# First block's scores from on-chip operands over 64 rows each, and six search steps planned among the weight conversions

## Chip, core and metric

One core of one Trainium2 chip runs the whole program. The metric is the device time of one execution in microseconds (us); smaller is better. The engines are called as the profile calls them: PE (TensorE), ACT (ScalarE), DVE (VectorE), POOL (GpSimd), and SP (SyncE), which here issues every DMA. A profiled execution supplies the trace.

## What is computed

Attention over 4 batches, 8 heads, 576 tokens and head size 64 keeps only the 32 largest scores of each row. Its output goes through two dense layers.

```python
scores = scale * np.matmul(q, k.transpose(0, 1, 3, 2))
kth = np.partition(scores, -32, axis=-1)[..., -32:-31]
scores = np.where(scores >= kth, scores, -1000000000.0)
attn = softmax(scores)                      # max subtracted, exp, divided by the sum
x = (attn @ v) as [2304 tokens, 512]
h = x @ w_in;  g = np.maximum(0.01 * h, h);  y = g @ w_out          # d_ff 2048
z = np.maximum(np.maximum(y @ w1, y @ w2), y @ w3) @ moe2_w_out     # d_ff 768
```

The weights arrive as 64-bit floats and are converted on the chip. The matrix operands are split into two 16-bit parts, a high and a low one, to keep the precision.

## The kernel before

**Search steps.** A batch is cut into four blocks of 128 query rows (F0 to F3) and one of 64 (HB). A step takes one pair of heads for a full block, or two pairs for HB, so a batch has 18 steps and the kernel has 72, numbered from 0 here. Batch 0 goes F0 (steps 0 to 3), HB (4 and 5), F1 (6 to 9), F2 and F3 (10 to 17). In a step, PE makes two tiles of scores (L707) in the single PSUM tile `s`. ACT copies each to `S` (L712), of which there are three buffers. DVE searches the 32 largest with eight MAX8 (L722) and six MATCH_REPLACE8 (L724). ACT and POOL then make the exponentials `pp` and their 16-bit parts `phl` (L746 to L754), a DMA transposes `phl` into `pt` (L757), and PE multiplies by the values (L783 to L785). `pp`, `phl` and `pt` have one buffer each. The result of a block is transposed by another DMA into `xu` (L819), the input of the dense layers.

**Operands of the scores.** `prep_qk` loads q and k of a pair of heads, scales them, splits them into `hl` (in batch 0 in the tile `ph`, which lies where the weights `wo` will be, so the trace calls it `wo`) and writes both parts to DRAM (`dqk`, L394). `load_k` and `load_q` read them back (L411, L419, L422) in an order that puts the high and the low part of the 64 components on 128 rows.

**Dense units.** The 2304 tokens form ten units: unit 0 is F0 and HB of batch 0, unit 1 is F1, unit 2 is F2 with F3, and so on. A unit has four matrix phases on PE: H (`h<-xu,wi`), Y (`acc<-f16t,wo`), M (`h<-k,w`) and O (`acc<-f16t,w`). H of unit 0 needs all of w_in and w_out; M of unit 0 needs all of w1 to w3 and moe2_w_out.

**Conversions.** w_in and w_out come in eight chunks each of 1 MB (`raw` tile with three buffers, L490). DVE turns a chunk's two pieces into 32-bit floats with three operations each (L501, L504, L507); ACT and POOL then scale and split it. w1 to w3 and moe2_w_out (`rw`) follow.

**The order.** Each engine's program is fixed ahead by `Plan.run`, a list scheduler with a cost per operation. An operation has a priority; that of step i is `TP(i)`, which is `TE + TS*i` for the first `NE` steps and `10 + 11.9*i` after them. The chunks of weights have priorities from 2.0 upwards, 2.1 apart for w_in, then 1.5, 1.7 and 1.5. Every engine runs its list in order, so an operation that waits holds up all behind it.

Of the kernel before, what the change touches and what calls it, by code (L numbers as in the profile page):

```python
# [10 lines left out]
F16 = mybir.dt.float16  # L11
# [3 lines left out]
AF = mybir.ActivationFunctionType  # L15
# [3 lines left out]
B, H, S, D = 4, 8, 576, 64  # L19
# [10 lines left out]
P = 128  # L30
# [8 lines left out]
ORDER = [[F0, HB, F1, F2, F3], [F0, F1, F2, F3, HB], [HB, F0, F1, F2, F3], [F0, F1, F2, F3, HB]]  # L39
# [10 lines left out]
PD = 0.0  # L50
WEPS = 0.03
WEPS2 = 0.03
NE = 4
TE = 0.0
TS = 2.0
DSH = 0.6
SLACK = 0.4
START = 4.0
# [2 lines left out]
class Buf:  # L61
    def __init__(self, tag, make):
        self.tag, self.make, self.ap, self.left, self.seq, self.also = tag, make, None, 0, None, ()
        self.done, self.emit = None, 0
        self.last = 0.0

    def __call__(self):
        return self.ap
# [6 lines left out]
class Plan:  # L75
# [50 lines left out]
    def run(self):  # L126
        free = {e: 0.0 for e in (PE, ACT, DVE, POOL, SP)}
        dma_free, landed = 0.0, 0.0
        lanes = [0.0] * 8
        slots = {t: [0.0] * n for t, n in self.nbufs.items()}  # L130
        nexts = {t: 0 for t in self.nbufs}
        pend = {e: [] for e in free}
        order = []
        for n in self.nodes:
            if n.nd == 0:
                pend[n.eng].append(n)
        total = len(self.nodes)
        while len(order) < total:
            best = None
            for e, lst in pend.items():  # L140
                t0 = free[e]
                cand = None
                for n in lst:
                    t, ok = max(n.ready, t0, lanes[-8] if e == SP else 0.0), True
                    need = {}
                    for b in n.bufs:
                        if b.ap is None and b.last == 0.0 and not getattr(b, "on", False):
                            k = need.get(b.tag, 0)
                            sl = slots[b.tag]
                            if len(sl) <= k or (b.tag not in self.free_order and b.seq != nexts[b.tag] + k):  # L150
                                ok = False
                                break
                            need[b.tag] = k + 1
                            t = max(t, sl[k] + 0.2)
                    if not ok:
                        continue
                    key = (max(t - n.eps, t0), n.pr, n.idx)
                    if cand is None or key < cand[0]:
                        cand = (key, n, t)
                if cand is not None and (best is None or cand[2] < best[2]):  # L160
                    best = cand
            if best is None:
                raise RuntimeError("no instruction can go on")
            _, n, t = best
            pend[n.eng].remove(n)
            for b in n.bufs:
                if not getattr(b, "on", False):
                    b.on = True
                    slots[b.tag].sort()
                    slots[b.tag].pop(0)  # L170
                    nexts[b.tag] = max(nexts[b.tag], b.seq + 1)
            end = t + n.dur
            if n.eng == SP and n.dur > 1.0:
                free[SP] = max(end, landed + 0.15)
                end = free[SP] + n.dma
                dma_free = max(dma_free, end - 0.9)
            elif n.eng == SP:
                free[SP] = end
                st = max(t + 1.1, dma_free)
                dma_free = st + DSH * n.dma  # L180
                end = st + 0.95 * n.dma + (START if t < 10.0 else 0.9)
            else:
                free[n.eng] = end
            if n.eng == SP:
                end += SLACK
                landed = max(landed, end)
                lanes.append(end)
            order.append((t, n.idx))
            for b in n.bufs:
                b.left -= 1  # L190
                b.last = max(b.last, end)
                if b.left == 0:
                    slots[b.tag].append(b.last)
                    slots[b.tag].sort()
            for m in n.succ:
                m.nd -= 1
                m.ready = max(m.ready, end + self.LAT.get((n.eng, m.eng), 0.2) + m.lag)
                if m.nd == 0:
                    pend[m.eng].append(m)
        order.sort()  # L200
        for _, i in order if self.EMIT else ():
            n = self.nodes[i]
            for b in n.bufs:
                if b.ap is None:
                    b.ap = b.make()
            n.fn()
            for b in n.bufs:
                b.emit -= 1
                if b.emit == 0 and b.done:
                    b.done()  # L210
# [6 lines left out]
def act(n, psum=False, aps=0):  # L217
    return (n * 0.833 + (52 if psum else 94) + 93 * aps) / 1000
# [10 lines left out]
def dma(nbytes):  # L229
    return nbytes / 255e3  # L230
# [3 lines left out]
def attention_moe_kernel(ctx, tc, qk, v, w_in, w_out, w123, w2o, outT):  # L234
# [137 lines left out]
    def prep_qk(b, hp, pr, fast):  # L372
        d = dr.tile([2, 2, 2, D, S], F16, name=f"dqk{b}_{hp}")
        use_ring(("qk", b % 2, hp), 10)
        bi = col(2)
        kb = ("es", b, hp)
        for a in (1, 0):
            key = ("qk", b, hp, a)
            z0 = ["ZO"] if b == 0 else [] if b == 1 else ZL
            raw = buf("raw" if b else "pr", [P, 768])  # L380
            if b:
                raw.also = (plan.buf("rc", lambda: 1),)
            op(SP, 0.55, lambda raw=raw, a=a: Y.dma_start(raw()[:, :S], qk[b, hp, a]), w=[raw] + ([("l1", hp, a)] if b == 1 else []),
               r=z0 + (GQ if b == 0 and hp > 1 else []), pr=pr,
               dma=dma(P * S * 4))
            n2 = col()
            square(lambda raw=raw: raw()[:, :S], S, n2, [raw] + z0, [(key, "n2")], pr)
            n2s = total([n2], [(key, "n2")], pr)
            s, _ = pow2(key, lambda n2s=n2s: n2s()[:, :1], 1, [n2s], pr, b=bi[:, a:a + 1])
            hl = buf("hl" if b else "ph", [P, 2, S], F16)  # L390
            split3(lambda raw=raw: raw()[:, :S], s, lambda hl=hl: hl()[:, 0], lambda hl=hl: hl()[:, 1], S,
                   [raw, (key, "s")] + z0, [(hl, 0), (hl, 1)], pr, DVE if fast else POOL)
            for h in range(2):
                op(SP, 0.55, lambda hl=hl, a=a, h=h: Y.dma_start(d[a, h].rearrange("r d s -> d r s"),  # L394
                                                               hl()[h * D:(h + 1) * D]),
                   r=[(hl, 0), (hl, 1)] + z0, w=[("d", b, hp, a, h)], pr=pr, dma=dma(P * S * 2))
        es, es2 = col(), col()
        op(POOL, 0.32, lambda: G.tensor_tensor(es, bi[:, 0:1], bi[:, 1:2], op=ALU.mult),
           r=[(("qk", b, hp, a), "b") for a in range(2)], w=[(kb, 0)], pr=pr)
        op(POOL, 0.32, lambda: G.tensor_scalar(es2, es, 0.125, 2.0 ** -54, op0=ALU.mult, op1=ALU.max),  # L400
           r=[(kb, 0)], w=[(kb, 1)], pr=pr)
        ES[b, hp] = es2
        use_ring()
        return d

    GQ = []
    DQK = {}

    def load_k(b, hp, pr):
        k = buf("kt", [P, 2, S], F16)  # L410
        op(SP, 0.55, lambda: Y.dma_start(k(), DQK[b, hp][1].rearrange("h r d s -> (r d) h s")),  # L411
           r=[("d", b, hp, 1, 0), ("d", b, hp, 1, 1)], w=[k], pr=pr, dma=dma(P * 2 * S * 2))
        KT[b, hp] = k

    def load_q(b, hp, t0, n, pr):
        q = buf("qt", [P, 2, 2, P], F16)
        rd = [("d", b, hp, 0, 0), ("d", b, hp, 0, 1)]
        src = DQK[b, hp][0]
        op(SP, 0.55, lambda: Y.dma_start(q()[:, :, 0, :n], src[:, :, :, t0:t0 + n].rearrange("h r d s -> (r d) h s")),  # L419
           r=rd, w=[(q, 0)], pr=pr, dma=dma(P * 2 * n * 2) + 0.2)  # L420
        for r in range(2):
            op(SP, 0.55, lambda r=r: Y.dma_start(q()[r * D:(r + 1) * D, :, 1, :n],  # L422
                                                src[:, 1 - r, :, t0:t0 + n].rearrange("h d s -> d h s")),
               r=rd, w=[(q, 1 + r)], pr=pr, dma=dma(P * n * 2) + 0.2)
        QT[b, hp, t0] = q

    SV, BX, V0 = {}, {}, []

    def v_stats(b, pr):
# [255 lines left out]
    def attention(i):  # L685
# [7 lines left out]
        pr -= PB  # L693
        Sp, wp, m = buf("S", [P, 2, S]), buf("w", [P, 2, S]), buf("m", [P, 2, TOPK])
        Sb = [lambda j=j: Sp()[:, j] for j in range(2)]
        for j in range(2):
            k, q = KT[b, hps[j]], QT[b, hps[j], t0]
            p = buf("s", [P, 2, 512])
            hs = [(j, slice(0, P))] if full else [(0, slice(0, 64)), (1, slice(64, P))]
# [443 lines left out]
```

## Time and profile before

| | |
|---|---|
| median of 3 runs | 1080.87 us (1079.48 to 1082.93) |
| profiled execution | 1078.56 us; its span, first to last instruction, 1076.6 us |
| PE busy | 903.1 us (84%) |
| DVE busy | 875.2 us (81%) |
| ACT busy | 835.2 us (78%) |
| POOL busy | 600.5 us (56%) |

The shares are averages over stages. The program begins with DMA, conversions and searches, while PE has little to do; from the first dense units on, PE has work nearly all the time. Idle time of an engine matters only where something that ends the program waits for it.

### The profile page before, as it was taken

How to read it: one execution, taken by the hardware profiler on the slowest of the kernel's cores; microseconds unless marked ns; L12 is line 12 of the kernel's file. 1: busy time of each engine (PE TensorE's matmuls, PEld its weight loads, DVE VectorE, ACT ScalarE, POOL GpSimd, SP SyncE). 2: the span in 40 equal slices, each digit the busy share in tenths (PEclk: the TensorE clock that was granted, in tenths of full speed). 3: DMA queues.
4: the chain of work that ended last, by engine and by line, in shares of the span. 5: the costliest groups of instructions: out<-in, count | busy, mean ns of one | idle time of the engine just before them, and what ended most of it. 6: DMA issues, size and time to landing. Idle time of an engine off the chain costs nothing.

```text
span 1076.6 us, 27391 instructions
## 1 busy us (share of the span) xinstructions
PE 903.1 (84%) x10292; PEld 795.0 (74%) x10292; DVE 875.2 (81%) x2010; ACT 835.2 (78%) x1769; POOL 600.5 (56%) x1110
## 2 busy tenths in 40 slices
PE   3343334688999998998999899989999999999998
PEld 2231223577988887887888798878878897888998
DVE  5899999999998999999459999999389999900101
ACT  7777878999888888689879868987887788664242
POOL 5355766776476655467655545666754555443131
PEclk9985556789999999999999999999999999999999
DMA  8968447547755443355763334663833343220000
GB/s 283 310 147 277 162 110 247 158 111 150 129 106 118 100 89 68 77 125 127 143 173 82 80 76 98 155 123 88 173 80 88 79 90 85 65 60 2 21 2 16
DMA packets 268516, 125.78 MB, mean 117 GB/s; under 512 B 237408, under 2 KB 255328, under 8 KB 266336
## 3 DMA queue, kind: packets, MB, share of 16 engines
q1 hardware_dynamic: 268384, 124.04, 47.4%
q8 instruction: 81, 1.33, 0.5%
q14 instruction: 51, 0.42, 0.1%
HBM read 62.65 MB, written 14.16 MB: 71 GB/s over the span
## 4 chain that ended last, share of the span: by engine, by line
PE 42%; ACT 18%; DVE 10%; DMA 7%; POOL 6%; issue 5%; SPq 1%; POOLq 0%; ACTq 0%; DVEq 0%
PE h L825 7%; PE h L826 7%; PE h L827 7%; PE acc L825 5%; PE acc L826 5%; PE acc L827 5%; DMA pt<-phl 3%; DVE m L722 3%; PE s L707 3%; POOL phl L754 3%; DVE w L724 3%; ACT pp L749 3%; ACT pp L746 2%; ACT S L712 2%; DMA raw<-in_v 2%
## 5 line engine op out<-in xcount | busy, mean ns | idle before, releaser
L722 DVE MAX8 m<-w 128x8 f32<-128x576 f32 x432 | 308.8, 748 | 0.3
L886 POOL TENSOR_TENSOR f16t<-k,f16t 128x256 f16<-128x256 f32 (+2 forms) x220 | 136.9, 624 | 211.2 <-ACT f16t L880 193.1
L754 POOL TENSOR_TENSOR phl<-pp,phl 128x576 f16<-128x576 f32 x144 | 183.5, 1282 | 85.3 <-ACT phl L752 83.2
L724 DVE MATCH_REPLACE8 w<-m,w 128x576 f32<-128x576 f32 x288 | 212.4, 743 | 0.0
L825 PE MATMUL h<-k,w 128*128 128x256 f16 (+2 forms) x720 | 186.4, 263 | 7.7 <-ACT k L926 5.5
L826 PE MATMUL h<-k,w 128*128 128x256 f16 (+2 forms) x720 | 186.3, 263 | 3.4 <-POOL k L928 3.0
L827 PE MATMUL h<-k,w 128*128 128x256 f16 (+2 forms) x720 | 186.3, 263 | 0.0
L826 PE MATMUL acc<-f16t,wo 128*128 128x256 f16 (+2 forms) x640 | 165.8, 263 | 3.7 <-POOL f16t L886 3.7
L825 PE MATMUL acc<-f16t,wo 128*128 128x256 f16 (+2 forms) x640 | 166.0, 263 | 0.7 <-ACT f16t L880 0.6
L827 PE MATMUL acc<-f16t,wo 128*128 128x256 f16 (+2 forms) x640 | 165.9, 263 | 0.0
L825 PE MATMUL h<-xu,wi 128*128 128x256 f16 (+1 forms) x576 | 155.9, 271 | 3.2 <-DMA xu<-xhl 1.9
L827 PE MATMUL h<-xu,wi 128*128 128x256 f16 (+1 forms) x576 | 156.0, 271 | 0.0
L826 PE MATMUL h<-xu,wi 128*128 128x256 f16 (+1 forms) x576 | 156.0, 271 | 0.0
L707 PE MATMUL s<-kt,qt 128*128 128x288 f16 (+5 forms) x800 | 106.2, 281 | 46.1 <-ACT S L712 31.8
L746 ACT ACTIVATE pp<-S,nt 128x576 f32<-128x576 f32 x144 | 107.9, 771 | 32.7 <-POOL nt L732 24.8
L880 ACT ACTIVATE f16t<-k 128x256 f16<-128x256 f32 (+2 forms) x220 | 86.9, 396 | 56.3 <-DVE k L970 53.7
L749 ACT ACTIVATE pp<-pp,nb,colt 128x576 f32<-128x576 f32 x144 | 123.7, 866 | 0.1
L722 DVE MAX8 m<-S 128x8 f32<-128x576 f32 x144 | 103.5, 746 | 19.1 <-ACT S L712 19.0
L707 PEld LDWEIGHTS <-qt 128*128 128x128 f16 (+1 forms) x800 | 62.3, 106 | 66.3 <-issue 41.9
L873 ACT ACTIVATE k<-h,colt 128x256 f32<-128x256 f32 (+2 forms) x160 | 72.4, 455 | 48.0 <-PE h L827 47.4
L826 PEld LDWEIGHTS <-w 128*128 128x128 f16 x960 | 94.2, 98 | 17.4 <-issue 9.2
L724 DVE MATCH_REPLACE8 w<-m,S 128x576 f32<-128x576 f32 x144 | 106.4, 743 | 0.0
(132 smaller groups left out, 2507.6 us busy)
## 6 DMA issues: line engine op xcount, KB each, us to landing
rw<-in_w SPq DMA_DIRECT2D x18, 512.0 KB, 5.5
w<-in_w_in SPq DMA_DIRECT2D x8, 1024.0 KB, 7.2
w<-in_w_out SPq DMA_DIRECT2D x8, 1024.0 KB, 5.6
raw<-in_qk SPq DMA_DIRECT2D x24, 288.0 KB, 3.5
dqk<-hl SPq DMA_DIRECT2D x48, 144.0 KB, 2.7
kt<-dqk SPq DMA_DIRECT2D x16, 288.0 KB, 3.0
qt<-dqk SPq DMA_DIRECT2D x144, 32.0 KB, 2.2
raw<-in_v SPq DMA_DIRECT2D x12, 352.0 KB, 3.4
```

Of the source, the lines that this page charges most:

```text
L707: T.matmul(p()[osl, h, o:o + w], q()[:, hh, st, :n], k()[:, hh, kc:kc + w], start=st == 0, stop=st == 1, skip_group_check=True)
L722: op(DVE, dve(S), lambda mc=mc, src=src: V.max(mc(), src()), r=rd, w=[(m, j, 0, r)], pr=pd)
L724: op(DVE, dve(S) + 0.06, lambda mc=mc, src=src, j=j: V.match_replace(out=wp()[:, j], in_to_replace=mc(), in_values=src(), imm_value=NEG), ...
L746: op(ACT, act(S, aps=1), lambda j=j: A.activation(pp()[:, j], Sb[j](), AF.Prelu, bias=nt()[:, j:j + 1], alpha=STEEP), r=[(Sp, j), nt], w=[ ...
L749: op(ACT, act(S, aps=2), lambda j=j, es=es: A.activation(pp()[:, j], pp()[:, j], AF.Exp, bias=nb()[:, j:j + 1], scale=es), r=[(nb, j), ((" ...
L754: op(POOL, pool(S), lambda j=j: G.tensor_tensor(phl()[:, 1, j], pp()[:, j], phl()[:, 0, j], op=ALU.subtract), r=[(pp, j), (phl, 0, j)], w= ...
L825: T.matmul(out, wt(0), xt(0), start=first, stop=False, skip_group_check=True)
L826: T.matmul(out, wt(0), xt(1), start=False, stop=False, skip_group_check=True)
L827: T.matmul(out, wt(1), xt(0), start=False, stop=last, skip_group_check=True)
L873: op(ACT, act(N, True, 1), lambda: A.activation(rr()[:, 0, :N], p()[:, :N], AF.Prelu, scale=SC["e"][:, c:c + 1], alpha=0.01), r=[p, "e_in" ...
L880: op(ACT, act(N), lambda: A.activation(hl()[:, 0, :N], g()[:, 0, :N], AF.Copy), r=[(g, 0)], w=[(hl, 0)], pr=pr)
L886: op(POOL, pool(N), lambda: G.tensor_tensor(hl()[:, 1, :N], g()[:, 0, :N], hl()[:, 0, :N], op=ALU.subtract), r=[(g, 0), (hl, 0)], w=[(hl, ...
```

## The change

Four things change.

- In the first block of batch 0 (steps 0 to 3) the scores come from `hl` itself. Its 128 rows are two heads of 64 components, so each product is over 64 rows, and four products (high and low of q with high and low of k) replace two. k's `hl` takes a `kt` buffer, q's stays in `ph`. The read-back of k and q for this block is gone; k is read back when HB first needs it. The writes to DRAM stay, with a priority later by 8.
- `NE` goes from 4 to 6 and `TS` from 2 to 4. The priorities of steps 0 to 5 were 0, 2, 4, 6, 57.6 and 69.5 and are now 0, 4, 8, 12, 16 and 20.
- The planner remembers when a buffer's slot came free (`since`) and lets no later user of that buffer start before it.
- Each first-block step now has its two score tiles divided by columns of the keys, not by head, and each copy to `S` writes both heads.

```diff
-NE = 4
+NE = 6
 TE = 0.0
-TS = 2.0
+TS = 4.0
...
                             need[b.tag] = k + 1
                             t = max(t, sl[k] + 0.2)
+                        else:
+                            t = max(t, b.since)
...
-                    slots[b.tag].pop(0)
+                    b.since = slots[b.tag].pop(0) + 0.2
...
-            hl = buf("hl" if b else "ph", [P, 2, S], F16)
+            hl = buf("hl" if b else "kt" if a else "ph", [P, 2, S], F16)
+            if b == 0:
+                DIR[hp, a] = hl
+                if a:
+                    z0 = []
...
-                   r=[(hl, 0), (hl, 1)] + z0, w=[("d", b, hp, a, h)], pr=pr, dma=dma(P * S * 2))
+                   r=[(hl, 0), (hl, 1)] + z0, w=[("d", b, hp, a, h)], pr=pr + DP * (b == 0), dma=dma(P * S * 2))
...
     def load_k(b, hp, pr):
+        if b == 0 and hp not in KL:
+            KL.add(hp)
+            k_done.discard((b, hp))
+            return
...
     def load_q(b, hp, t0, n, pr):
+        if b == 0 and t0 == ORDER[0][0][0]:
+            return
...
-        for j in range(2):
+        direct = b == 0 and t0 == ORDER[0][0][0]
+        for c in range(2) if direct else ():
+            k, q = DIR[hps[0], 1], DIR[hps[0], 0]
+            p = buf("s", [P, 2, 512])
+            seg = ([(0, 0, 0, 288), (1, 0, 512, 64), (1, 64, 0, 224)], [(0, 0, 288, 288), (1, 0, 224, 288)])[c]
+
+            def qkd(p=p, k=k, q=q, seg=seg):
+                for x in range(2):
+                    for y in range(2):
+                        for h, o, kc, w in seg:
+                            hx = slice(D * h, D * h + D)
+                            T.matmul(p()[:, h, o:o + w], q()[hx, x, t0:t0 + n], k()[hx, y, kc:kc + w],
+                                     start=x + y == 0 and o == 0, stop=x + y == 2, skip_group_check=True)
...
```

Where this moves work: first the start of DVE's list. `acc` rows are conversions, `S` and `m` rows are the first search. Before:

```order
L507 SCALAR_TENSOR_TENSOR w_76<-w_76,acc_152 128x512
L507 SCALAR_TENSOR_TENSOR w_76<-w_76,acc_159 128x512
L339 TENSOR_SCALAR colt<-h_190 128x1
L501 TENSOR_SCALAR acc_207<-w_76 128x512
L501 TENSOR_SCALAR acc_212<-w_76 128x512
L504 SCALAR_TENSOR_TENSOR acc_207<-w_76,acc_207 128x512
L504 SCALAR_TENSOR_TENSOR acc_212<-w_76,acc_212 128x512
L339 TENSOR_SCALAR colt<-h_218 128x1
L507 SCALAR_TENSOR_TENSOR w_76<-w_76,acc_207 128x512
L339 TENSOR_SCALAR colt<-h_229 128x1
L507 SCALAR_TENSOR_TENSOR w_76<-w_76,acc_212 128x512
L537 TENSOR_REDUCE colt<-h_232 128x1
```

In the change, the same place of DVE's list:

```order
L521 SCALAR_TENSOR_TENSOR w_76<-w_76,acc_153 128x512
L521 SCALAR_TENSOR_TENSOR w_76<-w_76,acc_171 128x512
L341 TENSOR_SCALAR colt<-h_211 128x1
L753 MAX m_223<-S_183 128x8 x2
L755 MATCH_REPLACE w_230<-m_223,S_183 128x576 x2
L753 MAX m_223<-w_230 128x8 x2
```

The second chunk of w_in no longer stands ahead of the first search; it now follows the second search, steps 2 to 5 each follow two more chunks, and seven of w_out's chunks stand behind the sixth search. Second, SP's list around the chunks of w_out, before:

```order
L757 DMA_TRANSPOSE pt_780<-phl_732 128x18x128
L490 DMA w_76<-in_w_in 128x1024
L422 DMA qt_765<-dqk_2_81 64x2x128
L490 DMA w_76<-in_w_out 128x1024 x3
L819 DMA_TRANSPOSE xu_921<-xhl_502 128x8x128
L490 DMA w_76<-in_w_out 128x1024 x5
L490 DMA rw_1321<-in_w 128x512
```

In the change, the second half of that stretch:

```order
L850 DMA_TRANSPOSE xu_1017<-xhl_535 128x8x128
L504 DMA w_76<-in_w_out 128x1024
L435 DMA qt_1007<-dqk_3_82 64x2x128
L788 DMA_TRANSPOSE pt_1048<-phl_1005 128x18x128
L504 DMA w_76<-in_w_out 128x1024
L432 DMA qt_1202<-dqk_0_79 128x2x128
L435 DMA qt_1202<-dqk_0_79 64x2x128 x2
L504 DMA w_76<-in_w_out 128x1024
L788 DMA_TRANSPOSE pt_1234<-phl_1190 128x18x128
L504 DMA w_76<-in_w_out 128x1024 x2
L850 DMA_TRANSPOSE xu_1017<-xhl_1103 128x8x64
```

One transpose stood among the eight loads of w_out; now four stand among them (that of step 3, not shown, and three of these). Third, DVE's list where the last pieces of moe2_w_out (tile `fl`) are converted, before:

```order
L722 MAX m_2155<-S_1447 128x8
L339 TENSOR_SCALAR colt<-colt 128x1
L501 TENSOR_SCALAR h_2161<-rw_2065 128x384
L722 MAX m_2155<-S_1447 128x8
L504 SCALAR_TENSOR_TENSOR h_2161<-rw_2065,h_2161 128x384
L724 MATCH_REPLACE w_2185<-m_2155,S_1447 128x576
L507 SCALAR_TENSOR_TENSOR fl_2140<-rw_2065,h_2161 128x384
```

In the change:

```order
L755 MATCH_REPLACE w_2619<-m_2547,w_2619 128x576
L518 SCALAR_TENSOR_TENSOR h_2823<-rw_2784,h_2823 128x384
L753 MAX m_2547<-w_2619 128x8
L521 SCALAR_TENSOR_TENSOR w_77<-rw_2784,h_2823 128x384
L515 TENSOR_SCALAR h_2846<-rw_2802 128x384
L753 MAX m_2547<-w_2619 128x8
L518 SCALAR_TENSOR_TENSOR h_2846<-rw_2802,h_2846 128x384
```

`m_2155` is the ninth search (step 8), `m_2547` the eleventh (step 10): the last conversion has moved behind two and a half more searches.

## Rows read from the trace of the kernel before

**Rows 1.** Windows: length, busy us (count) per engine, PE's granted clock, DMA share, GB/s.

```profile
0.00:22.48 22.48, 6.64 (x24) 5.17 (x25) 10.56 (x24) 16.23 (x32) 12.52 (x53) 1.00 0.87 297
22.48:65.30 42.82, 20.06 (x150) 12.37 (x149) 39.62 (x88) 34.84 (x60) 19.32 (x29) 1.00 0.82 241
65.30:126.20 60.90, 19.30 (x198) 13.36 (x197) 59.64 (x127) 46.62 (x68) 36.23 (x49) 0.55 0.77 242
126.20:316.70 190.50, 131.99 (x1674) 119.83 (x1671) 185.28 (x429) 167.70 (x359) 124.47 (x227) 0.79 0.59 141
316.70:349.10 32.40, 28.03 (x451) 25.81 (x452) 29.51 (x75) 29.27 (x67) 21.45 (x49) 0.95 0.52 107
349.10:1076.60 727.50, 697.05 (x7802) 618.47 (x7802) 550.61 (x1273) 540.52 (x1187) 386.48 (x705) 1.00 0.39 87
```

**Rows 2.** Timeline of PE: first matmuls of unit 0's H and M, unit 2's H.

```profile
186.66 0.34 PE L825 MATMUL h<-xu,wi 128*128 128x192 f16 x1 [1.52 <-DMA xu<-xhl]
...
258.42 0.25 PE L825 MATMUL h<-k,w 128*128 128x192 f16 x1
...
349.10 0.28 PE L825 MATMUL h<-xu,wi 128*128 128x256 f16 x1 [0.35 <-DMA xu<-xhl]
```

**Rows 3.** Way from step 17's search to unit 2 (timelines of DVE, ACT, SP).

```profile
315.91 0.74 DVE L722 MAX8 m<-w 128x8 f32<-128x576 f32 x1
...
323.79 1.43 ACT L746 ACTIVATE pp<-S,nt 128x576 f32<-128x576 f32 x2
327.44 0.68 ACT L752 ACTIVATE phl<-pp 128x576 f16<-128x576 f32 x1 [0.68 <-DMA pt<-phl]
...
346.16 1.24 SPq L819 DMA_TRANSPOSE xu<-xhl  x1
```

**Rows 4.** The first operands by way of DRAM (timelines of DVE and SP).

```profile
6.39 1.55 DVE L362 SCALAR_TENSOR_TENSOR wo<-wo,colt 128x576 f16<-128x576 f32 x2 [0.38 <-ACT wo L361]
...
7.34 2.79 SPq L394 DMA_DIRECT2D dqk<-wo  x4
...
21.95 0.42 DVE L537 TENSOR_REDUCE colt<-h 128x1 f32<-128x256 f32 x1 [1.29 <-PE h L532]
...
22.48 0.76 DVE L722 MAX8 m<-S 128x8 f32<-128x576 f32 x1
```

**Rows 5.** End of a square on ACT, first scores on PE, a copy on ACT.

```profile
10.29 0.19 ACT L354 ACTIVATION_READ_ACCUMULATOR junk<-wo 128x1 f32 x1
...
20.32 1.16 PE L707 MATMUL s<-kt,qt 128*128 128x288 f16 x4
...
23.65 0.65 ACT L712 ACTIVATE S<-s 128x576 f32<-128x576 f32 x1
```

**Rows 6.** Later scores: a full step's first tile, and an HB step's.

```profile
319.21 0.65 PE L707 MATMUL s<-kt,qt 128*128 128x288 f16 x4
...
542.24 0.69 PE L707 MATMUL s<-kt,qt 128*64 128x288 f16 x8
```

**Rows 7.** Loads of v on SP and DVE's wait for their norms.

```profile
31.51 1.56 SPq L440 DMA_DIRECT2D wo<-in_v  x3
...
45.59 0.16 DVE L444 TENSOR_REDUCE colt<-h 128x1 f32<-128x4 f32 x1 [3.13 <-PE h L325]
```

**Rows 8.** DVE's conversions, 65.3 to 126.2 us, grouped: busy, mean ns | idle before.

```profile
L507 DVE SCALAR_TENSOR_TENSOR w<-w,acc 128x512 int32<-128x512 int32 x28 | 19.0, 678 | 0.0
...
L501 DVE TENSOR_SCALAR acc<-w 128x512 int32<-128x512 int32 x28 | 18.1, 684 | 1.2 <-DMA w<-in_w_in 1.2
```

**Rows 9.** Transposes on SP, and the page's time to landing of a chunk.

```profile
45.29 6.59 SPq L757 DMA_TRANSPOSE pt<-phl  x1
...
58.87 1.97 SPq L757 DMA_TRANSPOSE pt<-phl  x1
...
w<-in_w_out SPq DMA_DIRECT2D x8, 1024.0 KB, 5.6
```

**Rows 10.** POOL's last split of the converted weights.

```profile
219.37 1.64 POOL L367 TENSOR_TENSOR w<-fl,w 128x768 f16<-128x768 f32 x1 [2.13 <-ACT w L366]
```

More of the change, by code (lines that the diff above doesn't have):

```diff
@@ L64, in __init__ @@
         self.done, self.emit = None, 0
-        self.last = 0.0
+        self.last = self.since = 0.0
     def __call__(self):
@@ L389, in prep_qk @@
             s, _ = pow2(key, lambda n2s=n2s: n2s()[:, :1], 1, [n2s], pr, b=bi[:, a:a + 1])
-            hl = buf("hl" if b else "ph", [P, 2, S], F16)
+            hl = buf("hl" if b else "kt" if a else "ph", [P, 2, S], F16)
[3 more added lines that the diff above has]
+                    z0 = []
             split3(lambda raw=raw: raw()[:, :S], s, lambda hl=hl: hl()[:, 0], lambda hl=hl: hl()[:, 1], S,
-                   [raw, (key, "s")] + z0, [(hl, 0), (hl, 1)], pr, DVE if fast else POOL)
+                   [raw, (key, "s")] + (["ZO"] if b == 0 else z0), [(hl, 0), (hl, 1)], pr, DVE if fast else POOL)
             for h in range(2):
@@ L406, in attention_moe_kernel @@
     GQ = []
-    DQK = {}
+    DQK, DIR = {}, {}
+    DP = 8.0
     def load_k(b, hp, pr):
+        if b == 0 and hp not in KL:
+            KL.add(hp)
+            k_done.discard((b, hp))
+            return
         k = buf("kt", [P, 2, S], F16)
@@ L425, in load_q @@
         QT[b, hp, t0] = q
+    KL = set()
     SV, BX, V0 = {}, {}, []
@@ L695, in attention @@
         Sb = [lambda j=j: Sp()[:, j] for j in range(2)]
-        for j in range(2):
+        direct = b == 0 and t0 == ORDER[0][0][0]
[10 more added lines that the diff above has]
+                                     start=x + y == 0 and o == 0, stop=x + y == 2, skip_group_check=True)
+            op(PE, 0.5 * COLD, qkd, r=[(k, 0), (k, 1), (q, 0), (q, 1), "ZO"], w=[p], pr=pq)
+            op(ACT, act(S, True), lambda c=c, p=p: A.activation(Sp()[:, :, 288 * c:288 * c + 288], p()[:, :, :288],
+                                                               AF.Copy), r=[p], w=[(Sp, 0), (Sp, 1)], pr=pq)
+        for j in range(2) if not direct else ():
             k, q = KT[b, hps[j]], QT[b, hps[j], t0]
```

## The prediction

> **What bounds the kernel now.** I read the windows first, cut at moments that the timelines gave: the first search, the end of the fourth, the start of the fifth, the end of step 17's search, and the start of unit 2. After 349.10 us PE is busy 697.05 of 727.50 us; DVE only 550.61 [rows 1]. From unit 2 on, then, PE sets the pace, and what moves unit 2's start moves the end by the same amount as long as nothing else changes. Before it PE is far from full (19.30 of 60.90 us between 65.3 and 126.2), and DVE is full: its idle time up to 316.70 us is 22.48−10.56 = 11.9, then 3.2, 1.3 and 5.2 us, together 21.6 us [rows 1].
>
> Next, what starts unit 2. Its first matmul, at 349.10 us, waited for the transpose into `xu` [rows 2], issued at 346.16 us, and that goes back to step 17's search, which ended at 315.91+0.74 = 316.65 us [rows 3]. So unit 2 starts 32.4 us after DVE has finished eighteen searches and all conversions. These are the same instructions before and after the change; only their order differs. That sum of DVE's work is my reason for caution: unit 0's H can start long before its 186.66 us [rows 2], but unit 2 cannot start before DVE has done it all. What the change can give is therefore DVE's idle time up to step 17, and the 32.4 us behind it.
>
> **The change, part by part.**
>
> *The first search.* q and k of the first heads are split at 6.39+1.55 = 7.94 us. They then go to DRAM (writes from 7.34 us) and back, and the search begins at 22.48 us [rows 4]. Now the scores follow at once. Four full matmuls of 288 columns, 1152 in all, took 1.16 us [rows 5]; a tile over 64 rows has 2304 columns by the diff (four products of 288, 64 and 224, then four of two times 288). Taken one after the other that is about 2.2 us. The first tile ends at 10.1 us. ACT has three squares ahead of the copy, the last ending at 10.5 us [rows 5]; the copy takes 0.65 us. PE's list has three totals between the two tiles, so the second starts at about 11.2, ends at 13.4, and its copy at 14.0 us. The search begins there, 8.5 us earlier. But DVE had converted the second chunk ahead of it, and now has not: two pieces with three operations of (19.0+18.1)/56 = 0.66 us each [rows 8] are 4.0 us, and its column reduction 0.42 [rows 4]. At 14.0 us DVE has then worked 10.56−4.4 = 6.1 us, so the idle time falls from 11.9 to 7.9: **−4.0 us**. Bounds: the search begins at 16 us if the tiles and squares collide (−2.0), at 12 if the two halves of rows run side by side (−6.0).
>
> The 2304 extra columns of each first-block step cost 2 x 1.1 us of PE, four times 2.2. PE is busy only 6.64 of the first 22.48 us and 20.06 of the next 42.82 [rows 1], which hides them; without that cover they would be 8.8 us. The trace has no product over half the rows, but it has products with half the columns: eight of them took 0.69 us where four whole ones took 0.65 [rows 6], so two halves ran side by side. The Trainium skill says the same of rows (TensorEngine Tiling (Array Packing), section Theoretical Speedup: up to twice the speed for a contraction of at most 64), and by that the first search would come 2 us earlier, term −6.0. [...]
>
> *The norms of v.* DVE waited 3.13 us for them at 45.59 us [rows 7]. Seven fewer DMAs stand ahead of v's loads, so 31.51 us [rows 7] becomes some 4 us earlier. But ACT now has two steps' copies and the first exponentials ahead of v's squares, and DVE reaches the reduction earlier too, five operations after the second search. I take **0**, with bounds −3.1 (the wait goes) and +2.
>
> *Chunks between searches.* Each chunk now has a search of some 10 us beside it, so early loads have slack. The price is at the end: seven chunks of w_out stand close together behind the sixth search, with four transposes among their loads on SP where one stood. A transpose held SP 6.59 us while loads were in flight, and 1.97 us when none were [rows 9]. The last two loads stand behind step 5's. At worst 6.6 us of holding and 5.6 us to landing, less two converted chunks in hand at 4.0 each, is 4.2 us of waiting, at one place; with 1.97 us it is nothing. Before, such waits were 1.2 us in all [rows 8]. Between the ends I take **+1.7**; bounds 0 and +6 (two places of the worse kind). The Trainium skill has a rule that would make this nothing (DMA: Bandwidth & Descriptors, section Rules for kernel authors: "A transpose next to ordinary DMAs needs nothing"). It speaks of safety; by it as a time, the term is 0 and the sum 1.7 us lower. The row of 6.59 us disagrees, and I follow the row.
>
> *w1 to w3 and moe2_w_out* come later on DVE, behind two and a half more searches. Unit 0's M needs them. The last split ended at 219.37+1.64 = 221.0 us [rows 10], M began at 258.42 [rows 2]; 25 us later is 244 with the gain so far, still 14 us ahead. No cost: the cover is the 37 us between the two. Step 17's search needs the same DVE work, so it does not move by this.
>
> *Behind step 17.* The exponential began at 323.79 us, 7.1 us after its search; then `phl` waited for the transpose before it [rows 3]. So ACT, POOL and the one `pt` were behind. In the change steps 6 to 10 are spread between conversions, and the backlog starts later; M and O of unit 0 come earlier and take less of ACT there. I take **−2.5**, bounds 0 and −7.1 (no backlog at all).
>
> *The planner's `since`* and the later writes to DRAM change the order, not the amount of work; both are in the lists above, 0.
>
> Sum: −4.0 + 0 + 1.7 + 0 − 2.5 = −4.8 us. The profiled execution took 1078.56 us (span 1076.6 and 2.0 around it), so it becomes 1073.8; it was 2.3 us below the median of 1080.87, which becomes **1076.1 us**.
>
> **Rivals.**
>
> *Unit 2 follows PE, not DVE.* If the 32.4 us are elastic and M of unit 0 at 244 instead of 258.42 carries all behind it, the gain is 14 us: 1067. For it: PE is busy 28.03 of the 32.40 us before unit 2 [rows 1], so the two limits are nearly equal. Against it: step 17's search would have to end, or its way to `xu` be, 14 us shorter. Chance 0.12.
>
> *The first unit's start decides.* All of w_out was converted by 126 us; with two searches ahead of it, 20 us and 4 more for its split, H could start at about 150 instead of 186.66 [rows 2], 36 us: 1045. Against it: M's weights, and DVE's total. Chance 0.02.
>
> *No change within 0.3%.* The on-chip scores do not come earlier, or the four microseconds are given back at v's norms or at w_out: 1078 to 1084. Here falls the case that the change does not do what it says: the tiles wait for squares and totals, and the search begins only at 16 us. Chance 0.27.
>
> *Slower.* The transposes hold SP while DVE waits for chunks. Five that stand near w_out's loads, at 2.5 to 3 us of DVE's time each, are 13 us; less 4.0 it is +9: 1090. It decides from a DVE wait of more than 4.0+2.5+3.2 = 9.7 us in that stretch. For it: the row of 6.59 us [rows 9] and a DMA share of 0.77 there [rows 1]. Against it: DVE needs a chunk only every 4 us, and three buffers are ahead. Chance 0.21.
>
> **How the numbers follow.** The forecast has 0.38, on its own 1073 to 1077.6. A measurement of this kernel can tell about 0.3% (3.2 us) from no change. Faster: 0.38+0.12+0.02 = 0.52; same 0.27; slower 0.21. The range holds the second rival's 1067, and reaches above to 1087, all bounds on the bad side (−2.0, +2, +6, 0: +6.0); it leaves out the whole gain of unit 0 and the worse half of the slower case.
>
> **What the changed profile would show.** The first MAX8 at 14 us (12 to 16). A wait at the reduction of v's norms, now about 40 us, of some 3 us. DVE's idle time up to step 17's end: 8 + 3 + 3 + 5 = 19 to 20 us, against 21.6. Unit 0's H at about 150 us and its M at 244, with PE waiting in between. Step 17's search ending at 314 to 315 us, unit 2 at 344 to 345, and then 727 us of PE to the end. The prediction is wrong if unit 2's H moves by more than DVE's searches do, if the 727.5 us change, or if DVE waits over 10 us for chunks of w_out.

## The result, and the profile after

The changed kernel took 1072.18 us (median of 4 runs, 1067.32 to 1074.41) where the kernel before took 1081.9 beside it (4 runs, 1079.48 to 1085.5). The ratio is 0.9915, with a 95% interval of 0.9888 to 0.9943: faster by 6 to 12 us. The profiled execution has a span of 1069.8 us against 1076.6, so 6.8 us less. The profiled execution of before lay 3.3 us below its median here, that of after at its own; that is the rest of the 9.7 us between the medians. In three later sets of runs, of 29, 11 and 21 executions, the median of the kernel before was 1080.5, 1080.5 and 1080.0 us, so 1081.9 may be some 1.5 us high and the gain nearer 8 us than 9.7.

The windows of the changed kernel (columns as in [rows 1]), cut at the first search, the end of step 3's search, 126.20 us as before, the end of step 17's search and the start of unit 2. Here 126.20 us is only a time and no event: DVE converts w_out until 141.3 us.

```profile
0.00:14.21 14.21, 5.83 (x32) 4.15 (x32) 6.01 (x15) 9.06 (x19) 5.57 (x41) 1.00 0.87 313
14.21:75.90 61.69, 25.86 (x200) 15.85 (x201) 55.89 (x123) 53.03 (x89) 35.93 (x52) 1.00 0.93 256
75.90:126.20 50.30, 20.35 (x208) 14.25 (x206) 50.30 (x110) 36.06 (x59) 25.59 (x42) 0.91 0.61 166
126.20:315.10 188.90, 136.19 (x1736) 124.64 (x1736) 183.09 (x423) 172.66 (x370) 130.12 (x238) 0.82 0.59 157
315.10:345.46 30.36, 23.86 (x362) 21.92 (x360) 28.44 (x70) 27.53 (x57) 19.31 (x39) 0.84 0.55 126
345.46:1069.80 724.34, 696.28 (x7803) 619.76 (x7801) 550.92 (x1275) 538.15 (x1180) 383.21 (x700) 0.99 0.39 87
```

Three differences make up the 6.8 us. DVE's idle time (window less the third busy column) up to step 17's end is 8.2 + 5.8 + 0 + 5.8 = 19.8 us where it was 21.6, and that search ends at 315.1 instead of 316.7: 1.6 us. From there to unit 2 it is 30.36 instead of 32.40: 2.0 us. This stretch is called the hand-over below. From unit 2 to the end it is 724.3 instead of 727.5: 3.2 us, of which PE's idle time is 2.4.

The start, from the timelines of PE (score tiles), ACT (their copies to `S`) and DVE:

```profile
8.37 0.66 PE L721 MATMUL s<-kt,wo 64*128 64x288 f16 x6 [1.87 <-ACT wo L363]
9.22 0.66 PE L721 MATMUL s<-kt,wo 64*128 64x288 f16 x6 [0.19 <-DVE wo L364]
...
12.34 1.14 PE L721 MATMUL s<-kt,wo 64*128 64x288 f16 x8
...
11.66 0.63 ACT L725 ACTIVATE S<-s 128x576 f32<-128x576 f32 x1
...
13.52 0.65 ACT L725 ACTIVATE S<-s 128x576 f32<-128x576 f32 x1
...
14.21 1.42 DVE L753 MAX8 m<-S 128x8 f32<-128x576 f32 x2
```

The first tile was done at 9.9 us, but ACT had three squares to do first, which held its copy until 11.66. The second tile needs the same PSUM tile, so it began behind that copy. Eight products over 64 rows took 1.14 us, as long as four over 128 in [rows 5].

The wait for the norms of v, the conversions between 75.9 and 126.2 us (grouped, idle time last), and three of the four transposes that now stand among w_out's loads on SP (the fourth, of `xu`, held SP for 1.26 us):

```profile
39.73 0.16 DVE L458 TENSOR_REDUCE colt<-h 128x1 f32<-128x4 f32 x1 [2.65 <-PE h L327]
...
L515 DVE TENSOR_SCALAR acc<-w 128x512 int32<-128x512 int32 x16 | 10.3, 675 | 0.0
...
86.06 4.89 SPq L788 DMA_TRANSPOSE pt<-phl  x1
...
105.03 3.57 SPq L788 DMA_TRANSPOSE pt<-phl  x1
...
120.89 5.42 SPq L788 DMA_TRANSPOSE pt<-phl  x1
```

These three held SP for 3.6 to 5.4 us each, and DVE still never waited for a chunk: it was busy 50.30 of 50.30 us, and from there to the end of w_out at 141.3 us it had no wait for one either.

The start of unit 2, from the timelines of SP and PE:

```profile
340.63 1.24 SPq L850 DMA_TRANSPOSE xu<-xhl  x1
...
342.68 1.12 PE L738 MATMUL s<-kt,qt 128*128 128x64 f16 x6 [2.12 <-ACT S L743]
344.55 1.12 PE L738 MATMUL s<-kt,qt 128*128 128x288 f16 x4 [0.75 <-ACT S L743]
345.46 0.42 PE L856 MATMUL h<-xu,wi 128*128 128x256 f16 x1
```

`xu` was issued 5.5 us earlier than in [rows 3], but unit 2's first matmul came only 3.6 us earlier than in [rows 2]. It no longer waits for `xu`. Two score tiles stand ahead of it in PE's list, and both waited for ACT, which was busy 27.53 of the 30.36 us. Before, 2.94 us lay between the issue of `xu` and unit 2's first matmul; by that `xu` was ready at about 343.6 us here (an estimate), 1.9 us before it was used.

### The profile page after: what moved, and what is told of

It is laid out like the page before. It is cut to its first block, busy times and chain, and to the rows that moved or that the text cites. A ratio compares the mean times of both kernels' runs of the same rounds, so it can differ in the third digit from the quotient of the medians.

```text
span 1069.8 us, 27427 instructions
## 1 busy us (share of the span) xinstructions
PE 908.4 (85%) x10332; PEld 800.6 (75%) x10332; DVE 874.7 (82%) x2010; ACT 836.5 (78%) x1769; POOL 599.7 (56%) x1110
## 4 chain that ended last, share of the span: by engine, by line
PE 48%; ACT 15%; DVE 10%; issue 5%; POOL 4%; DMA 3%; SPq 1%; POOLq 0%; ACTq 0%; DVEq 0%
PE h L856 8%; PE h L857 8%; PE h L858 8%; DVE m L753 5%; PE acc L856 5%; PE acc L857 5%; PE acc L858 5%; DVE w L755 4%; PE s L738 4%; ACT pp L777 2%; ACT pp L780 2%; ACT S L743 2%; DMA pt<-phl 2%; PE h L814 1%; PE h L815 1%
## 5 line engine op out<-in xcount | busy, mean ns | idle before, releaser
L738 PE MATMUL s<-kt,qt 128*128 128x288 f16 (+5 forms) x760 | 99.8, 282 | 43.7 <-ACT S L743 38.0
L857 PEld LDWEIGHTS <-w 128*128 128x128 f16 x960 | 94.6, 99 | 19.2 <-issue 10.9
L858 PEld LDWEIGHTS <-w 128*128 128x128 f16 x960 | 94.6, 99 | 14.6 <-issue 6.8
```

Of the source, the lines that this page charges most:

```text
L738: T.matmul(p()[osl, h, o:o + w], q()[:, hh, st, :n], k()[:, hh, kc:kc + w], start=st == 0, stop=st == 1, skip_group_check=True)
L857: T.matmul(out, wt(0), xt(1), start=False, stop=False, skip_group_check=True)
L858: T.matmul(out, wt(1), xt(0), start=False, stop=last, skip_group_check=True)
```

## Experiments

The theories, as the texts on record call them. **D**, the prediction's: unit 2 and the end follow DVE's idle time up to step 17, and the hand-over behind it. **P**: the end follows units 0 and 1 on PE. **A**: ACT's and PE's lists in the last 30 us start unit 2. **L**: the way the lists (the order of each engine's instructions) fit together behind step 17 makes the difference. Ratios are to the kernel before, with 95% intervals; each table of windows shows the program up to step 17's end, from there to unit 2, and from unit 2 to the end.

### Which part gives it

```diff
-NE = 4
+NE = 6
...
-TS = 2.0
+TS = 4.0
```

> The kernel before with NE = 6 and TS = 4.0 only; the first block's operands still go by way of DRAM. Theory D (the prediction's: unit 2 and the end follow DVE's idle time up to step 17, and the hand-over behind it): the first search stays at 22.5 us and about 12 us of DVE's early idle time stay, so only the hand-over term is left, 2 to 4 us: 1078 to 1080 where the kernel before has 1082. Theory P (the gain is that units 0 and 1 come earlier on PE, since steps 4 and 5 no longer wait for all of w_out): units 0 and 1 move by some 10 us as in the changed kernel, and the time with them: 1072 to 1074. Rival Z: the numbers without the earlier scores are worth nothing or cost: 1082 or more.

Measured: 1087.98 us, ratio 1.0066 (1.0047 to 1.0085). Slower, as only Z had it.

```profile
0.00:24.20 24.20, 6.63 (x24) 5.16 (x25) 10.61 (x24) 16.20 (x32) 12.48 (x53) 1.00 0.81 275
...
0.00:321.10 321.10, 190.67 (x2135) 162.11 (x2136) 295.52 (x666) 271.26 (x533) 195.87 (x368) 0.78 0.65 183
321.10:354.10 33.00, 23.75 (x392) 21.84 (x389) 31.82 (x79) 28.16 (x60) 21.32 (x44) 0.87 0.50 118
354.10:1086.20 732.10, 698.67 (x7775) 619.91 (x7772) 549.04 (x1268) 538.87 (x1178) 381.80 (x699) 0.99 0.40 86
```

DVE was idle for 25.6 us before step 17's end, 4 more than before, and the last stretch is 4.6 us longer; the hand-over is 0.6 us longer, where D had it 2 to 4 shorter. Unit 0 began 26 us earlier than before (160.2 us) and unit 1's O ended 6 us earlier (342.4), without use: P falls.

The scores alone are the changed kernel with the two numbers set back. That keeps the rest of the change with them (the tiles divided by columns, the later writes to DRAM), which no run takes apart.

```diff
-NE = 6
+NE = 4
...
-TS = 4.0
+TS = 2.0
```

> The changed kernel with NE = 4 and TS = 2.0 as before, so the scores of the first block come from on-chip operands, but steps 4 and 5 keep their late priorities. Theory D: the first search starts at 14 us, DVE's early idle time falls by 4 us, the hand-over stays as before: 1077 to 1079. Theory P: units 0 and 1 start about where they did before (187 and 284 us), so nothing is gained: 1081 to 1083. If the two parts add up, this one and the one with the numbers alone give together the 9.7 us of the whole change.

Measured: 1076.25 us, ratio 0.9966 (0.9950 to 0.9982), 3.7 us faster than before. The profiled execution lay at the top of its range (1073.64 to 1080.38).

```profile
0.00:15.50 15.50, 5.84 (x32) 4.20 (x32) 6.20 (x15) 9.14 (x19) 5.88 (x41) 1.00 0.86 309
...
0.00:313.40 313.40, 180.18 (x2098) 151.05 (x2099) 294.45 (x664) 265.35 (x518) 192.04 (x357) 0.81 0.66 186
313.40:348.00 34.60, 28.25 (x469) 26.29 (x466) 32.80 (x82) 31.86 (x74) 24.92 (x54) 0.95 0.54 110
348.00:1078.60 730.60, 699.11 (x7777) 620.95 (x7773) 548.26 (x1267) 535.34 (x1179) 381.66 (x699) 0.99 0.39 87
```

Step 17's search ended 3.3 us earlier than before, 2.6 of them by DVE's idle time (19.0 against 21.6 us), as D says. But D had the rest unchanged, and here the hand-over is 2.2 us longer and the last stretch 3.1: this execution lost behind step 17 more than it had won, so its windows do not show where the 3.7 us of the median come from. The parts don't add up: +7 and −4 give +3, together they gave −9. Some twelve us are in how the two meet. The third edit, `since`, is no part of it: the changed kernel has the same list on every engine with and without it.

### DVE's work before step 17

```diff
...
+                    def mx(mc=mc, src=src):
+                        V.max(mc(), src())
+                        if i == 12:
+                            V.max(mc(), src())
...
```

> The changed kernel in which each of the eight MAX8 of step 12 is issued twice with the same result: 8 times 0.75 us = 6.0 us more for DVE before step 17, nothing else. Theory D: the search of step 17 ends at 321 instead of 315 us, unit 2 starts at 351 to 352 and the end is 6 us later: 1078 where the changed kernel has 1072. Theory A (what starts unit 2 is ACT's and PE's lists in the last 30 us, where ACT was busy 27.57 of 30.40 us, not DVE): half or more is absorbed, 1072 to 1075. Theory P: PE sets unit 2 by the end of unit 1's O, 1072 to 1074.

Measured: 1075.94 us, ratio 0.9959 (0.9945 to 0.9973).

```profile
0.00:317.50 317.50, 189.40 (x2170) 159.22 (x2171) 301.05 (x675) 270.31 (x534) 196.99 (x372) 0.88 0.65 184
317.50:347.80 30.30, 23.80 (x363) 22.01 (x361) 28.38 (x70) 27.47 (x57) 19.29 (x39) 0.84 0.56 127
347.80:1073.10 725.30, 696.65 (x7803) 619.81 (x7801) 551.10 (x1275) 537.42 (x1180) 382.22 (x700) 0.99 0.38 87
```

Step 11's search ended at 247.7 us in this execution, 2.1 earlier than in that of the changed kernel, and step 17's 2.4 later; so 4.5 of the 6.0 us came through, and unit 2 moved by the same 2.4. With this list the distance from step 17 on is the same. The time lies between D's 1078 and the 1072 to 1075 of A.

```diff
-                    op(DVE, dve(S), lambda mc=mc, src=src: V.max(mc(), src()), r=rd, w=[(m, j, 0, r)], pr=pd)
+                    ml = S // 2 if 10 <= i < 18 and g else S
+                    op(DVE, dve(S), lambda mc=mc, src=src, ml=ml: V.max(mc(), src()[:, :ml]), r=rd,
+                       w=[(m, j, 0, r)], pr=pd)
```

> The changed kernel in which steps 10 to 17 search only the first 288 of the 576 columns in the second to fourth MAX8 of each row (48 instructions), so the 9th to 32nd largest come from half the scores; that part of the computation is left out. By the spread between conversions of 512 and 384 columns (0.68 and 0.55 us) that takes about 0.29 us off each, 14 us of DVE in all before step 17. Theory D: unit 2 moves with step 17's search until PE takes over; O of unit 1 ended 7.1 us before unit 2, so 5 to 8 us come through: 1064 to 1067. Theory A (ACT's and PE's lists start unit 2): 1070 to 1072, and DVE waits for scores instead, its idle time in 126 to 315 us growing by 8 us or more. If DVE alone counted, 1058.

Measured: 1071.49 us, ratio 0.9926 (0.9904 to 0.9947): no gain. The windows, and then DVE's waits from 240 to 313.3 us (in total, times, longest):

```profile
0.00:313.30 313.30, 186.81 (x2165) 157.53 (x2166) 281.93 (x666) 270.05 (x532) 196.55 (x372) 0.88 0.68 186
313.30:345.50 32.20, 25.72 (x369) 23.46 (x368) 28.58 (x71) 28.28 (x60) 19.40 (x40) 0.82 0.53 119
345.50:1071.80 726.30, 697.54 (x7803) 619.24 (x7801) 551.34 (x1275) 537.62 (x1180) 382.24 (x700) 0.99 0.38 87
```

```profile
DVE k L1003 <- PE h L860: 3.3, 5, 1.3
DVE colt L341 <- PE acc L968: 3.3, 2, 2.9
DVE r L823 <- ACT pp L782: 2.5, 1, 2.5
```

DVE had 13.4 us less work up to step 17's end and was idle 11.6 us longer, waiting for PE and ACT (its waits from 240 us on were 2.1 us in the changed kernel); unit 2 stayed at 345.5. This is what A expected, and D's 1064 to 1067 is missed. Extra work of DVE counts here, saved work does not: the engines are level there.

### PE and ACT

```diff
...
+                def hk(k=k, f=f, p=p):
+                    for _ in range(8 if u == 1 and k == 0 else 0):
+                        T.matmul(p()[:, :N], wi[:, 0, k, f * P:(f + 1) * P], xu()[:, 0, k, :N],
+                                 start=True, stop=False, skip_group_check=True)
...
```

> The changed kernel in which the first product of each of the sixteen H tiles of unit 1 is issued eight times more with the same result (128 extra products of 128 columns; such products follow each other at 0.055 us in the trace, so 7.0 us of PE before unit 2). Theory D: O of unit 1 ended 7.1 us before unit 2 began, so this is hidden: 1072 to 1073. Theory P: 1079. Theory A: PE was busy 37.42 of 40.40 us during that H, and what ACT does next waits for it, so 3 to 7 us come through: 1075 to 1079.

Measured: 1077.59 us, ratio 0.9975 (0.9956 to 0.9994).

```profile
0.00:319.80 319.80, 194.10 (x2301) 164.99 (x2302) 295.68 (x667) 271.41 (x534) 197.04 (x372) 0.79 0.66 182
319.80:350.10 30.30, 23.80 (x361) 21.83 (x358) 28.39 (x70) 27.45 (x57) 19.23 (x39) 0.84 0.55 127
350.10:1075.30 725.20, 698.17 (x7804) 620.64 (x7801) 551.21 (x1275) 537.87 (x1180) 382.26 (x700) 0.99 0.38 87
```

PE's extra work delayed step 17's search by 4.7 us (DVE idle 24.1 against 19.8) and unit 2 by 4.6. The slack of 7.1 us behind unit 1's O hid none of it, because the loss had already happened ahead of step 17. D, which had all of it hidden, is missed. A's size was right (3 to 7 us), but the place is ahead of step 17, not behind it.

```diff
+            def ph0(j=j):
+                for _ in range(3 if 16 <= i <= 18 else 1):
+                    A.activation(phl()[:, 0, j], pp()[:, j], AF.Copy)
...
```

> The changed kernel in which the six copies of the exponentials' high parts in steps 16 to 18 are each issued three times with the same result: 12 copies of 0.6 us, 7 us more for ACT in the last 40 us before unit 2. Theory D as the prediction had it (what stands behind step 17 is ACT's and POOL's backlog, and it sets unit 2): 4 to 7 us come through, unit 2 at 349 to 352, 1076 to 1079. If ACT is not what sets the hand-over but the transposes and PE's list are: 0 to 2 us, 1072 to 1074, hidden in ACT's idle time (2.8 us in the 30.4 us before unit 2) and in the wait of PE for unit 2's input.

Measured: 1079.95 us, ratio 1.0002 (0.9986 to 1.0018): the whole gain is gone.

```profile
0.00:315.20 315.20, 188.87 (x2168) 159.32 (x2169) 295.15 (x667) 272.30 (x536) 197.05 (x372) 0.77 0.67 185
315.20:352.50 37.30, 25.63 (x364) 23.09 (x363) 28.80 (x71) 34.23 (x67) 19.39 (x39) 0.82 0.56 103
352.50:1077.80 725.30, 696.59 (x7803) 619.94 (x7801) 551.14 (x1275) 537.72 (x1180) 382.18 (x700) 0.99 0.38 87
```

Step 17's search did not move; the hand-over grew from 30.4 to 37.3 us, nearly one for one with ACT's 6.7 us more (34.23 against 27.53). More work of ACT makes the hand-over longer; less work of ACT was not tried.

### The lists

> The kernel before, unchanged, for a second profile. If the three stretches of the first profile (up to step 17's search 316.7 us, from there to unit 2 32.4 us, from unit 2 to the end 727.5 us) belong to the kernel, theory L expects the last two again within 1.5 us, and what differs between executions to lie in the first 250 us, where the loads of the weights are. If single executions scatter by several us in the last stretch too, the 724 to 726 us of the changed kernel's list say nothing.

```profile
0.00:318.50 318.50, 180.23 (x2039) 152.36 (x2039) 295.40 (x664) 265.37 (x517) 191.62 (x357) 0.77 0.67 184
318.50:351.40 32.90, 28.04 (x451) 25.83 (x451) 29.36 (x76) 29.23 (x67) 21.56 (x50) 0.95 0.59 109
351.40:1079.80 728.40, 697.26 (x7802) 618.38 (x7802) 550.79 (x1275) 541.22 (x1187) 385.75 (x705) 1.00 0.39 87
```

Measured: 1081.83 us, one run. The hand-over (32.9 against 32.4 us) and the last stretch (728.4 against 727.5) belong to the kernel; single executions differ by about 2 us ahead of step 17.

```diff
-TS = 4.0
+TS = 3.5
```

> The changed kernel with TS = 3.5 instead of 4.0. PE's list is the same as the changed kernel's for its last 9640 of 10254 instructions; only the first block's surroundings differ. Theory D (DVE up to step 17, hand-over behind it): 1071 to 1074 where the changed kernel has 1072, for the same first search at 14 to 15 us. Theory L (a good part of the gain is how the order behind step 17 happens to fit together, so it goes with the list): the same 1071 to 1074 here, since the list behind is the same, and unit 2 to the end takes 724 to 726 us.

Measured: 1069.82 us, ratio 0.9911 (0.9891 to 0.9931), the lowest here, but not to be told from the changed kernel's 0.9915. D and L expected the same, so this run does not decide between them.

```diff
-TS = 4.0
+TS = 4.5
```

> The changed kernel with TS = 4.5 instead of 4.0. The first search stays alone ahead, one more chunk of w_in comes before the second, and the weights of w1 to w3 end behind step 12; PE's list is another one almost to the end (only the last 1159 instructions are the same). Theory D: DVE's work and its early idle time are those of the changed kernel, so 1071 to 1075. Theory L: unit 2 to the end takes 727 to 732 us, as in the kernel before (727.5), with the numbers alone (732.1) and with the scores alone (730.6), and not the 724 to 725 us of the three kernels that have the changed kernel's list: 1075 to 1083.

Measured: 1093.36 us, ratio 1.0135 (1.0111 to 1.0158). Both D and L are missed, L by 10 us. The windows of 3.5 and of 4.5, and from the second's timeline of PE the end of unit 1's O:

```profile
0.00:312.70 312.70, 188.33 (x2168) 159.98 (x2169) 294.84 (x667) 270.44 (x534) 196.97 (x372) 0.78 0.66 187
312.70:343.00 30.30, 23.98 (x365) 22.16 (x364) 28.43 (x70) 27.59 (x57) 19.34 (x39) 0.84 0.56 127
343.00:1067.10 724.10, 696.15 (x7803) 618.95 (x7801) 550.93 (x1275) 538.06 (x1180) 382.22 (x700) 0.99 0.38 87
```

```profile
313.90:350.40 36.50, 31.73 (x524) 29.80 (x521) 35.26 (x87) 31.54 (x76) 25.74 (x59) 0.95 0.49 99
350.40:1086.00 735.60, 699.95 (x7814) 621.01 (x7814) 546.14 (x1261) 536.80 (x1185) 384.00 (x701) 0.99 0.39 86
...
353.73 0.31 PE L858 MATMUL acc<-f16t,w 128*128 128x128 f16 x1
```

Half a unit in the spacing of the priorities costs 21 us by the medians. The profiled execution was the fastest of the six (1087.77 us), 15.8 us above that of the changed kernel. Step 17's search ended at 313.9 us, earlier than in the changed kernel, so DVE is not it. Unit 1's O ran until 354.0 us where the changed kernel had 338.4, so that unit 2 started before O had ended; the hand-over is 6 us longer and the last stretch 11.

```diff
-        return TE + TS * i if i < NE else TA0 + TA * i
+        return TE + TS * i if i < NE else TA0 + TA * i + (1.0 if i >= 24 else 0.0)
```

> The changed kernel with 1.0 added to the priority of steps 24 and later. PE's list is the changed kernel's for its first 4072 of 10254 instructions (to about 480 us), DVE's for its first 694 of 1245, and other lists behind. Theory D: no DVE or PE work is changed, PE sets the pace from unit 2 on, so unit 2 to the end stays at 724 to 726 us: 1071 to 1073. Theory L: unit 2 begins at 343 to 346 us as before this edit, but the stretch behind it is another one, 3 to 12 us longer as in the other lists (727.5, 730.6, 732.1, 735.6 us): 1075 to 1084.

> The same with 1.0 taken off the priority of steps 24 and later: PE's list the same for its first 4060 instructions. Theory D: 1071 to 1073. Theory L: another list again; if the changed kernel's is one of the well fitting ones, 1074 to 1084, if it is an ordinary one, 1065 to 1080.

Measured: 1076.86 us, ratio 0.9971 (0.9959 to 0.9983), and 1074.48 us, ratio 0.9946 (0.9928 to 0.9964). The last windows of the two:

```profile
345.10:1073.20 728.10, 697.27 (x7803) 620.67 (x7801) 552.11 (x1275) 537.58 (x1180) 382.74 (x700) 0.99 0.38 87
```

```profile
345.10:1071.80 726.70, 699.56 (x7803) 620.94 (x7801) 550.80 (x1275) 537.21 (x1180) 382.67 (x700) 0.99 0.38 87
```

Unit 2 starts where the changed kernel's does, and the first is slower by more than the intervals; the second can't be told apart. The seven kernels that share the changed kernel's list from behind the first block have 724.1 to 726.3 us behind unit 2, the seven executions with other lists 726.7 to 735.6 (two of them are of before). So another list with the same work can cost 3 to 4 us there, as L has it, and the 3 us of this change are of that size. Which waits in the list make them was not settled.

### The halves of the rows

```diff
-                for x in range(2):
-                    for y in range(2):
-                        for h, o, kc, w in seg:
+                for h, o, kc, w in seg:
+                    for x in range(2):
+                        for y in range(2):
```

> The changed kernel with the loops of the direct scores turned round: all four products of one half of the rows, then all four of the other, where the changed kernel alternates the halves. If two products over different halves run side by side only when they stand next to each other in PE's list, a tile of 2304 columns takes about 2.2 us instead of the 1.14 us of the changed kernel (0.5 ns a column, against 1.0 for four products over all 128 rows at the same place before): first search 1 to 2 us later, at 15 to 16 us, and by theory D up to 2 us on the end: 1072 to 1074. If the halves do not run side by side at all, the tile's time stays at 1.1 us and nothing moves.

Measured: 1071.41 us, ratio 0.9924 (0.9903 to 0.9944). The start of the first tile and the whole second tile, from PE's timeline:

```profile
7.24 0.66 PE L721 MATMUL s<-kt,wo 64*128 64x288 f16 x2 [1.33 <-ACT wo L363]
...
13.03 1.15 PE L721 MATMUL s<-kt,wo 64*128 64x288 f16 x8
```

The second tile took the same 1.15 us in this order of the list. The last expectation read that as a sign of no overlap, which was the wrong way round: 2304 columns in the time of 1152 in [rows 5] are two halves side by side, whichever order they are listed in. The first row is the check: two products of 288 columns over one half alone took 0.66 us, as long as the six over both halves, with twice the columns, at the same place of the changed kernel.

## Why the prediction was right, and where its terms were off

**The start (−4.0).** Measured −3.7 us of idle time (8.2 against 11.9); with the scores alone it was −2.6 (9.3). The first search came at 14.21, as worked out, but by luck, for two errors cancel. The prediction counted the columns of both halves in full, 2.2 us a tile, and no run shows that: the halves ran side by side, in 1.14 us. The Trainium skill (TensorEngine Tiling (Array Packing), section Theoretical Speedup) gives up to twice the speed for 64 rows; the trace agrees. And the copies on ACT came 1.2 us later than assumed, behind squares, and the second tile behind the first copy.

**The norms of v (0).** The wait was 2.65 us at 39.73, as expected. But DVE waited 1.3 us more in all from the first search to 126.2 us (5.8 against 4.5), within the term's bounds. 3.0 us of it are short waits for PE (the column norms of the chunks, the row sums of the exponentials) that no term had.

**Chunks (+1.7).** Mis-sized: 0. DVE never waited for w_out, though three transposes held SP for 3.6 to 5.4 us each. The rival "slower" falls with it. The Trainium skill's rule that a transpose next to ordinary DMAs needs nothing (DMA: Bandwidth & Descriptors, section Rules for kernel authors) is one of safety; taken as a time, it agrees with DVE's wait of 0 and not with the time that SP was held.

**w1 to w3 (0).** Unit 0's H began at 154.1 us and M at 248.8, for 150 and 244: later. POOL's last split ended at 249.5 us (221.0 before), 28 us later where the prediction had 25, so the cover of 37 us ahead of M was used up. It still cost nothing that the trace shows: O, which reads the last pieces, began at 258.0.

**The hand-over (−2.5).** Measured −2.0. ACT had 1.7 us less to do in it (27.53 against 29.27), and its extra copies show that ACT's work there counts in full. Why it had less is not shown: with the numbers alone steps 6 to 10 are spread as predicted, and the hand-over was 33.0 us. `xu` was issued 5.5 us earlier; PE's list put two score tiles ahead of unit 2 that waited for ACT.

**Step 17 and unit 2.** 315.1 and 345.5 us, for 314 to 315 and 344 to 345. That "unit 2 cannot start before DVE has done it all" held as a bound, and the distance behind step 17 was 30.3 to 30.4 us in five kernels with this list. One of its signs of being wrong did show, that unit 2 moves by more than DVE's searches do: 3.6 against 1.6 us. But the sum itself, with −2.5 behind step 17, had that. As the only bound it fell: with DVE relieved, PE and ACT held step 17 at 313.3.

**The step that was wrong: "then 727 us of PE to the end".** The prediction took PE's pace behind unit 2 as unchanged. The order behind it changed too, and gave 3.2 us in the profiles, 2.8 by the mean of the seven kernels with this list (725.2) against the two executions of before (728.0). By its own condition ("if the 727.5 us change") this step was wrong, in the direction that helped: that part of the gain is luck. The sum said −4.8 us and the profiles −6.8. The other errors (0.3, 1.3 and 0.5 us too hopeful, 0.6 us of idle time after 126.2 us that no term had, 1.7 too cautious) come to 1.0 us too hopeful, and DVE was busy 0.2 us longer; with the 3.2 us of this step that makes the −6.8.

**The rivals.** Unit 0's M came 9.6 us earlier than in [rows 2] and unit 1's O 10.3 (338.4 for 348.7), unit 2 only 3.6: neither rival in which PE's units carry the time came about, though PE holds step 17's search where work is added to it. "No change" falls by the interval, which ends at 0.9943.

**What stays open.** Why the numbers cost 7 us without the scores and bring 5 with them. Without the scores, the windows put 4.4 us ahead of step 17's end, 0.6 into the hand-over and 4.6 behind unit 2. With them, the numbers cost 1.7 us ahead of step 17's end and gain 4.2 in the hand-over and 6.3 behind unit 2, against an execution of the scores alone that was 4 us above its median. Which waits of the lists make this was not settled.

## What to carry to other kernels

A bound found in a busy engine can hold as a bound and still not be the only one. Test it in both directions: here the engines were level, added work cost time and saved work bought nothing. When a planner's numbers change, the order far behind the edit changes with them: try neighbouring values before a gain or a loss is put down to the edit. A constant stretch "to the end" is constant only for the same list.

## What was not expected of the hardware

Eight products over 64 rows each took 1.14 us and 1.15 us in two orders of the list, as long as four over 128 rows (1.16 us): the halves overlap without being listed alternately.

The column of PE's granted clock can't be read for the early stretch. [rows 1] has 1.00 there, yet four products of 288 columns took 1.16 us at 20.32 us [rows 5] and 0.65 us at 319.21 [rows 6]: PE ran at the lower of its two levels (1.2 GHz) while the column said 1.00. The same holds in the runs. From 0 to step 17's end the column has 0.78 with `TS` 3.5 and 0.88 with DVE's work cut, which looks like a faster clock in the second; in the window from 60 to 70 us it has 0.50 and 1.00. The same four products, in that window of the first and of the second:

```profile
65.35 1.12 PE L738 MATMUL s<-kt,qt 128*128 128x288 f16 x4 [0.35 <-ACT S L743]
...
66.95 1.12 PE L738 MATMUL s<-kt,qt 128*128 128x288 f16 x4 [0.34 <-ACT S L743]
```

They took 1.12 us in both, so the level was the same, and the difference between the two columns says nothing of the time.
